# Loading half of one batch's q in pieces of unequal height, in a sliding-window attention and spectral-mix kernel

## The chip, the cores and the metric

The kernel runs on one core of one Trainium2 chip. The metric is the device time of one execution, in microseconds. Five engines work side by side: TensorE (PE in the profile, with its weight loads as PEld), VectorE (DVE), ScalarE (ACT), GpSimd (POOL) and the sync engine (SP). Data come from HBM into SBUF by DMA transfers. Here GpSimd issues every transfer that converts float32 to bfloat16 on the way, and SP issues the first load of k and all stores. Sixteen DMA engines carry out the transfers.

## What is computed

q, k and v have 8 batches, 8 heads, 576 positions and 64 channels. A causal attention with a window of 64 positions gives x of 8 x 576 x 512. Then a Fourier mixing along the positions with 64 modes, each with two 512 x 512 float32 matrices, and a last channel product:

```python
    mask = (rel >= 0) & (rel < window)
    scores = np.where(mask, scores, -1000000000.0)
    ...
    return np.matmul(attn, v).astype(np.float32)
...
    X = np.fft.rfft(x, axis=1)
    Xr, Xi = (np.real(X[:, :n_modes]), np.imag(X[:, :n_modes]))
    Yr = np.einsum('bmd,mde->bme', Xr, w_r) - np.einsum('bmd,mde->bme', Xi, w_i)
    Yi = np.einsum('bmd,mde->bme', Xr, w_i) + np.einsum('bmd,mde->bme', Xi, w_r)
    Y[:, :n_modes] = Yr + 1j * Yi
    y = np.fft.irfft(Y, n=S, axis=1)
    u = x + y
    return (u + np.maximum(u @ w_ch, 0.0)).astype(np.float32)
```

The matrices `w_r` and `w_i` are 134 MB of float32, q, k and v together 28 MB. All of it is read from HBM once (the imaginary matrix of mode 0 is not needed).

## The kernel before

**Stages.** The attention runs first, batch after batch, in windows of 512 score columns (`NWIN` windows, the loop over `w`). While it runs, the first matrices of the mixing are loaded into every buffer that is free: `wls`, 13 early tiles, and then the attention's own buffers as they are given up (`spare`). At some 141 us the mixing begins: `half(i)` multiplies one 512 x 512 matrix with the spectra of all batches (line 618), and `issue(i)` loads the matrices that follow into a ring of buffers as they come free. The inverse transform and the channel product are laid between these steps. After the last matrix come the last products, additions and stores.

**The loads of q, k and v.** `load(b, which)` (lines 109 to 112) brings one batch's q, k or v into a raw tile of 128 partitions. `runs` (line 107) cuts the batch into 256 rows of 18 positions x 64 channels, 4,608 bytes of float32 each, and puts two of them, numbered by x, on each partition: row (g p) of the first four heads is x = 0, of the last four x = 1. There are two raw tiles of each kind, so the load of batch b + 2 waits for the transposes of batch b; `refill` places the loads and the early matrices in GpSimd's order. The last load of all is q of batch 7, and behind it on GpSimd stand matrices alone.

**The transposes.** `transpose_units(b)` turns the raw tiles by PE: `part` transposes six pieces of 64 channels for each x (line 247) into one PSUM tile, with `ident_bf` as the matrix that PE multiplies by, and copies the result out by ACT or DVE (line 58 or 59). The three units of q are the units 6, 7 and 8 of a batch.

**Order on the queues.** PE and GpSimd run in the order in which the program is written (`manual_schedule`); DVE and ACT are placed by the scheduler in the attention. GpSimd's transfers take eight completion semaphores in turn (DMASW0 to DMASW7 in the program's list of instructions). Each transfer waits, besides what its buffer asks for, for the semaphore that the transfer eight places earlier has used.

The lines that hold the loads of the matrices and the wait of the first q unit:

```python
        nc.gpsimd.dma_start(out=wt, in_=src[m].rearrange("(p c) e -> p c e", c=NC))
...
                        nc.tensor.transpose(out=ps[64 * hh:64 * hh + 64, c, :],
                                            in_=src[:, hh, (c0 + c) * D:(c0 + c + 1) * D],
                                            identity=ident_bf)
```

Of the kernel before, what the change touches and what calls it, by code (L numbers as in the profile page):

```python
# [11 lines left out]
BF16 = mybir.dt.bfloat16  # L12
# [8 lines left out]
def view(ap, off, dims):  # L21

    return bass.AP(ap.tensor, ap.offset + off, [list(ap.ap[0])] + [list(d) for d in dims])
# [3 lines left out]
def kernel(  # L27
# [10 lines left out]
    nc = tc.nc  # L38
    B, H, S, D = q.shape
# [8 lines left out]
    RUN = S // 32  # L48
# [6 lines left out]
    def evac(o, i, on_act):  # L55

        if on_act:
            return nc.scalar.copy(out=o, in_=i)  # L58
        return nc.vector.tensor_copy(out=o, in_=i)  # L59
# [10 lines left out]
    ident_bf = consts.tile([128, 128], BF16, name="ident_bf")  # L70
# [19 lines left out]
    acons = p1.enter_context(tc.tile_pool(name="acons", bufs=1, side="right"))  # L90
# [10 lines left out]
    RAW = {"k": k, "q": q, "v": v}  # L101

    def raw_tile(which):
        return rawp.tile([128, 2, RUN * D], BF16, name="r" + which)

    def runs(b, which):
        return RAW[which][b].rearrange("(x g) (p c) d -> (g p) x (c d)", g=4, c=RUN)

    def load(b, which):
        r = raw_tile(which)  # L110
        nc.gpsimd.dma_start(out=r, in_=runs(b, which))
        raws[b, which] = r


# [63 lines left out]
    with tc.manual_schedule(engines=ALL_FOUR):  # L178
# [3 lines left out]
        with tc.tile_pool(name="tmpf", bufs=1, side="right") as tmp:  # L182
            mo = tmp.tile([128, NM], FP32, name="mo")
            to = tmp.tile([128, NT], FP32, name="to")
            nc.gpsimd.iota(mo, pattern=[[1, NM]], base=0, channel_multiplier=0,
                           allow_small_or_imprecise_dtypes=True)
            nc.gpsimd.iota(to, pattern=[[128, NT]], base=0, channel_multiplier=1,
                           allow_small_or_imprecise_dtypes=True)
            nc.gpsimd.memset(ident, 0.0)
            nc.gpsimd.affine_select(out=ident, in_=ident, compare_op=ALU.not_equal, fill=1.0,  # L190
                                    base=0, pattern=[[-1, 128]], channel_multiplier=1)
            load(0, "q")
            load(0, "v")
            for t0, t1 in ((0, 3), (3, NT)):
                n = t1 - t0
                mt = tmp.tile([128, 2, n * NM], FP32, name="mtf")
                nc.vector.tensor_tensor(out=view(mt, 0, [[NM, n], [1, NM]]), in0=view(mo, 0, [[0, n], [1, NM]]),
                                        in1=view(to, t0, [[1, n], [0, NM]]), op=ALU.mult)
                gen_trig(tmp, mt, n * NM, trigF[:, t0:t1, 0:NM], trigF[:, t0:t1, NM:2 * NM], "f")
                if t0 == 0:  # L200
                    nc.vector.tensor_copy(out=ident_bf, in_=ident)
        nc.scalar.activation(out=spark, in_=ident[:, 0:1], func=ACT_F.Exp)
        raws[0, "k"] = raw_tile("k")
        for c, engine in enumerate((nc.vector, nc.gpsimd, nc.vector)):
            cc = slice(6 * D * c, 6 * D * (c + 1))
            engine.tensor_copy(out=raws[0, "k"][:, :, cc], in_=k_first[:, :, cc])
        load(1, "k")
        for i in range(4):
            half = i % 2
# [24 lines left out]
    def transpose_units(b):  # L234

        rk, rq, rv = (raws.pop((b, which)) for which in "kqv")
        qT = qtp.tile([128, 4, S], BF16, name="qT")
        vT = vtp.tile([128, 4, S], BF16, name="vT")
        kT, vt = kTs[b % 2], vts[b % 2]
        qTs[b] = qT  # L240

        def part(src, dst, c0, on_act):
            def f():
                ps = ps_misc.tile([128, 6, 128], BF16, name="pst", tag="misc")
                for c in range(6):
                    for hh in range(2):
                        nc.tensor.transpose(out=ps[64 * hh:64 * hh + 64, c, :],  # L247
                                            in_=src[:, hh, (c0 + c) * D:(c0 + c + 1) * D],
                                            identity=ident_bf)
                evac(view(dst, c0, [[S, 4], [RUN, 32], [1, 6]]),  # L250
                     view(ps, 0, [[32, 4], [1, 32], [128, 6]]), on_act)
            return f

        def vback(u):
            def f():
                ps = ps_misc.tile([128, 6, 128], BF16, name="psv", tag="misc")
                for i in range(6):
                    a, j = divmod(6 * u + i, 9)
                    if j == 4:
                        parts = [(0, 64, 2 * a, 512), (64, 64, 2 * a + 1, 0)]  # L260
                    else:
                        parts = [(0, 128, 2 * a + (j > 4), 128 * j - (j > 4) * S)]
                    for r0, n, g, t0 in parts:
                        nc.tensor.transpose(out=ps[r0:r0 + n, i, :],  # L264
                                            in_=vT[:, g, t0:t0 + n], identity=ident_bf)
                evac(view(vt, 6 * u * VW, [[18 * VW, 2], [VW, 6], [1, D]]),
                     view(ps, 0, [[D, 2], [128, 6], [1, D]]), u != 1)
                if u:
                    hs = slice(u - 1, u + 2, 2)
                    nc.vector.tensor_copy(out=vt[64:128, 1, hs, 1:9], in_=vt[64:128, 0, hs, 0:8])  # L270
                    nc.vector.tensor_copy(out=vt[0:64, 1, hs], in_=vt[0:64, 0, hs])
            return f

        return [part(rk, kT, 0, True), part(rk, kT, 6, False), part(rk, kT, 12, True),
                part(rv, vT, 0, False), part(rv, vT, 6, True), part(rv, vT, 12, False),
                part(rq, qT, 0, True), part(rq, qT, 6, False), part(rq, qT, 12, True),
                vback(0), vback(1), vback(2)]

    def head_of(n):
# [143 lines left out]
    with tc.manual_schedule(engines=ALL_FOUR):  # L423
        first = transpose_units(0)
        for j in (0, 1, 2, 6, 7, 8):
            first[j]()
            refill(0, j)
            if j in (2, 8):
                warm_up(3)
        for half in range(2):  # L430
            pp = slice(64 * half, 64 * half + 64)
            nc.vector.tensor_copy(out=band2[pp], in_=band[pp, half, :])
        mask(0, 1)
        scores(0)
        for j in (3, 4, 5):
            first[j]()
            refill(0, j)
            warm_up(2)
        for vt in vts:
            nc.vector.memset(vt[:, 0, :, :, 64:66], 1.0)  # L440
        for j in (9, 10, 11):
            first[j]()
            refill(0, j)
        nc.vector.memset(pso, 1.0)
        nc.vector.tensor_copy(out=ident_r, in_=ident)
    with tc.manual_schedule(engines={E.PE, E.Pool}):
# [9 lines left out]
        def unit(b, j):  # L456
            if b not in units:
                units[b] = transpose_units(b)
            units[b][j]()
            refill(b, j)  # L460
            turned(b, j)

        for w in range(NWIN + 1):
# [5 lines left out]
            n = len(todo)  # L469
# [16 lines left out]
            if w in (NWIN - 4, NWIN - 1):  # L486
                i = (B - 2) % 2 if w == NWIN - 4 else (B - 1) % 2
                spare(kTs[i])
                spare(qtp.tile([128, 4, S], BF16, name="qT"))
            if w in (NWIN - 4, NWIN):  # L490
                i = (B - 2) % 2 if w == NWIN - 4 else (B - 1) % 2
# [386 lines left out]
    for k, (f, delta, n, few) in enumerate(items):  # L878
        i = S_I + k * (T_I - 2 - S_I) // len(items)
# [25 lines left out]
    with tc.manual_schedule(engines=ALL_FOUR):  # L905
# [92 lines left out]
        for k in range(6):  # L998
# [10 lines left out]
                              in_=view(psys[0], 0, [[2 * B, NC], [2, B], [1, 2]]))  # L1009
# [78 lines left out]
```

## Time and profile before

| what | us |
|---|---|
| median of 3 runs | 425.69 (425.55 to 426.05) |
| the profiled execution | 425.65 |
| its span, first to last instruction | 423.8 |
| PE busy | 352.3 (83%) |
| DVE, ACT, POOL busy | 189.2, 159.8, 81.6 |
| weight loads of PE (beside its products) | 233.6 |
| last transfer of a matrix issued, landed | 375.98, 390.39 |

The span is divided into 40 slices of 10.6 us; the profile gives for each the busy share of every engine, the mean busy share of the sixteen DMA engines and the rate in bytes written. A transfer of 512 KB (bfloat16 as written) is one matrix, 1 MB of float32 as read. "To landing" is the time from an issue to the last of the transfer's sixteen completions, one from each DMA engine. The trace also holds each completion and each packet with its queue, start and size, but not its engine. The profiled run's granted clock of PE is 0.84 of full speed on the mean.

### The profile page before, as it was taken

What the parts mean: (1) busy time and instruction counts of PE and PEld (TensorE: products, weight loads), DVE (VectorE), ACT (ScalarE), POOL (GpSimd) and SP (SyncE); (2) the same over time, 40 slices, a digit from 0 to 9 for tenths busy, and PEclk for the clock granted to TensorE, in tenths of its full rate; (3) what the DMA queues carried; (4) which work ended last, traced back from release to release, by engine and by line L of the source; (5) the groups of instructions that cost most, each with busy time, mean ns of one, the idle gap of its engine ahead of it and who ended that gap; (6) DMA issues with size and microseconds to landing.
All of it is one profiled execution on the core that took longest, in us unless ns stands there. A gap on an engine that the chain in (4) does not pass through costs nothing.

```text
span 423.8 us, 11438 instructions
## 1 busy us (share of the span) xinstructions
PE 352.3 (83%) x5156; PEld 233.6 (55%) x5185; DVE 189.2 (45%) x359; ACT 159.8 (38%) x267; POOL 81.6 (19%) x146
## 2 busy tenths in 40 slices
PE   7799999999997779866669587767789899998994
PEld 3466656656654567644446455545556565554451
DVE  6676775766764001634332351121104345340895
ACT  5565766767754100122102110110023343330863
POOL 6322222221031130411112012120121112200000
PEclk9999999999999555966756656666579999999997
DMA  8999999999999999999999999999999999995598
GB/s 212 211 214 212 214 212 212 213 213 213 214 214 214 213 215 261 215 214 214 215 214 213 215 213 215 215 213 215 213 215 214 214 213 211 214 214 106 203 370 320
DMA packets 29920, 92.55 MB, mean 218 GB/s; under 512 B 2352, under 2 KB 2352, under 8 KB 29872
## 3 DMA queue, kind: packets, MB, share of 16 engines
q0 software_dynamic: 24624, 81.21, 95.9%
q1 hardware_dynamic: 5248, 10.62, 6.8%
q8 instruction: 40, 0.66, 0.6%
q14 instruction: 8, 0.07, 0.0%
HBM read 162.53 MB, written 9.44 MB: 406 GB/s over the span
## 4 chain that ended last, share of the span: by engine, by line
PE 42%; DMA 39%; DVE 7%; issue 5%; ACT 3%; POOL 0%; DVEq 0%; POOLq 0%; ACTq 0%
DMA wms<-in_moe_w_r_dram 20%; DMA wms<-in_moe_w_i_dram 19%; PE psy L618 7%; PE pso L343 6%; PE pst L247 5%; PE psv L264 3%; PE psx L365 3%; PE pss L963 3%; DVE x_sb L351 2%; PE pss L956 2%; PE pss L300 2%; PE pss L319 2%; PE psy L903 2%; DVE vT L59 2%; PE psf L800 1%
## 5 line engine op out<-in xcount | busy, mean ns | idle before, releaser
L759 PE MATMUL psz<-wch,xT 128*128 128x512 f32 x144 | 65.0, 594 | 0.0
L753 DVE CAST xT<-pxt 128x1024 fp32r<-128x1024 bf16 x18 | 22.0, 1224 | 78.0 <-PE pxt L748 78.0
L762 ACT CAST Z<-psz 128x1024 fp32r<-128x1024 f32 x18 | 18.2, 1012 | 102.2 <-PE psz L759 94.5
L325 ACT ACTIVATE et<-pss 128x512 bf16<-128x512 f32 x72 | 39.2, 599 | 13.7 <-PE pss L319 13.7
L618 PE MATMUL psy<-XQ,wls 128*128 128x16 bf16 x560 | 22.0, 192 | 23.7 <-DMA wls<-in_moe_w_r_dram 14.2
L759 PEld LDWEIGHTS psz<-wch,xT 128*128 128x128 f32 x144 | 37.4, 287 | 5.9
L618 PE MATMUL psy<-XQ,wms 128*128 128x16 bf16 x624 | 25.1, 192 | 17.9 <-DMA wms<-in_moe_w_i_dram 12.7
L618 PEld LDWEIGHTS <-wls 128*128 128x128 bf16 x560 | 19.5, 106 | 33.8 <-DMA wls<-in_moe_w_r_dram 17.4
L618 PEld LDWEIGHTS <-wms 128*128 128x128 bf16 x624 | 21.4, 103 | 30.2 <-DMA wms<-in_moe_w_i_dram 15.3
L343 PE MATMUL pso<-vt,et 128*64 128x65 bf16 (+1 forms) x576 | 32.3, 203 | 3.5 <-DVE x_sb L351 1.6
L811 DVE TENSOR_TENSOR Z<-pse,Z 128x1024 fp32r<-128x1024 f32 x16 | 19.6, 1225 | 29.3 <-PE pse L800 29.3
L343 PEld LDWEIGHTS <-et 128*64 128x64 bf16 (+1 forms) x576 | 22.2, 109 | 14.2 <-issue 6.7
L351 DVE TENSOR_TENSOR x_sb<-pso,rcp 128x640 bf16<-128x640 f32 x32 | 26.3, 822 | 0.9
L618 PE MATMUL psy<-XQ,wt 128*128 128x16 bf16 x560 | 20.5, 192 | 4.8 <-DMA wt<-in_moe_w_i_dram 2.3
L618 PEld LDWEIGHTS <-wt 128*128 128x128 bf16 x560 | 18.3, 104 | 11.2 <-DMA wt<-in_moe_w_i_dram 4.3
L59 DVE CAST YT<-psy 128x256 fp32r<-128x256 f32 x6 | 2.5, 424 | 42.0 <-PE psy L618 32.7
L59 DVE COPY vT<-pst 128x768 bf16<-128x768 bf16 x16 | 15.3, 958 | 12.9 <-PE pst L247 11.3
L981 ACT ACTIVATE pss<-pss 128x512 f32<-128x512 f32 x35 | 18.5, 581 | 4.7 <-PE pss L963 4.1
L300 PE MATMUL pss<-band,ident_bf 64*64 64x512 bf16 x120 | 16.5, 396 | 0.0
L264 PE MATMUL psv<-ident_bf,vT 128*128 128x128 bf16 (+1 forms) x160 | 15.6, 226 | 0.6 <-DVE vT L59 0.6
L58 ACT COPY vt<-psv 128x768 bf16<-128x768 bf16 x16 | 12.9, 807 | 8.3 <-PE psv L264 8.2
L58 ACT COPY qT<-pst 128x768 bf16<-128x768 bf16 x16 | 12.9, 813 | 6.4 <-PE pst L247 6.4
(191 smaller groups left out, 605.7 us busy)
## 6 DMA issues: line engine op xcount, KB each, us to landing
wt<-in_moe_w_i_dram POOLq DMA_DIRECT2D x19, 512.0 KB, 20.4
wt<-in_moe_w_r_dram POOLq DMA_DIRECT2D x16, 512.0 KB, 19.4
wls<-in_moe_w_r_dram POOLq DMA_DIRECT2D x8, 1024.0 KB, 21.8
wms<-in_moe_w_i_dram POOLq DMA_DIRECT2D x7, 1024.0 KB, 22.2
wms<-in_moe_w_r_dram POOLq DMA_DIRECT2D x7, 1024.0 KB, 21.6
wls<-in_moe_w_i_dram POOLq DMA_DIRECT2D x6, 1024.0 KB, 21.3
rq<-in_q_dram POOLq DMA_DIRECT2D x8, 576.0 KB, 15.3
rv<-in_v_dram POOLq DMA_DIRECT2D x8, 576.0 KB, 13.8
```

Of the source, the lines that this page charges most:

```text
L58: return nc.scalar.copy(out=o, in_=i)
L59: return nc.vector.tensor_copy(out=o, in_=i)
L247: nc.tensor.transpose(out=ps[64 * hh:64 * hh + 64, c, :], in_=src[:, hh, (c0 + c) * D:(c0 + c + 1) * D], identity=ident_bf)
L264: nc.tensor.transpose(out=ps[r0:r0 + n, i, :], in_=vT[:, g, t0:t0 + n], identity=ident_bf)
L300: nc.tensor.matmul(out=pss[(2 * w + hh) % 3][64 * half:64 * half + 64, :], lhsT=ident_bf[pp, pp], rhs=view(band[pp], 128 * half, [[0, WIN ...
L325: nc.scalar.activation(out=et[:, hh, :], in_=pss[(2 * w + hh) % 3], func=ACT_F.Exp, scale=EX_SCALE)
L343: nc.tensor.matmul(out=pso[po, hh, block(b, i // 2) * VW:block(b, i // 2) * VW + D + 1], lhsT=et[pk, hh, col:col + 64], rhs=vt[pk, 1 - f % ...
L351: nc.vector.tensor_tensor(out=view(x_sb, b * NT * DM + g * D, [[4 * D, 2], [DM, NT], [1, D]]), in0=view(pso, 0, [[512, 2], [VW, NT], [1, D]]),
L618: nc.tensor.matmul(out=view(psy, off + 2 * B * e, [[1, 2 * B]]), lhsT=w[:, c, 128 * e:128 * e + 128], rhs=XQ[:, m // HM, c, :, 1 - im:3 - ...
L753: nc.vector.tensor_copy(out=o, in_=i)
L759: nc.tensor.matmul(out=psz[s][:, j, :], lhsT=xts[s % 2][0][:, j, 128 * c:128 * c + 128], rhs=wch[:, c, :], start=(c == 0), stop=(c == NC - 1))
L811: nc.vector.tensor_tensor(out=z, in0=ps, in1=z, op=ALU.add)
```

## The change

The load of q of batch 7 (`BY_PARTS`) becomes eight transfers. The 128 rows of x = 0 are taken by six: (parts, rows of each part) are (5, 2), (2, 2), (2, 2), (4, 2), (3, 2) and (4, 24), with source rows dealt to the parts in turn, so that the rows land on the partitions in another order. A seventh, `aside`, brings 24 pieces of 16 values, as 12 parts of 2, into a tile that nothing reads. The eighth brings the 128 rows of x = 1 as before, in one. The transposes of batch 7's q for x = 0 use `back`, a matrix with the columns of `ident_bf` in the order that undoes the shuffle; six DVE copies build it. The list of instructions shows GpSimd with seven transfers more in the place of this load and else the same order, DVE with the six copies placed early, behind the second product of the first table of sines, PE with the same number of instructions, and the first q unit of batch 7 waiting for the six part transfers' semaphores and for that of the eighth transfer in place of one. Everything behind takes the semaphore one place earlier in the cycle of eight.

```diff
+    BY_PARTS = (B - 1, "q")
+    PARTS = ((5, 2), (2, 2), (2, 2), (4, 2), (3, 2), (4, 24))
+    REST = 12
+    assert sum(n * m for n, m in PARTS) == 128 and (sum(n for n, m in PARTS) + REST) % 16 == 0
+    aside = acons.tile([2 * REST, 16], BF16, name="aside")
+    back = acons.tile([128, 128], BF16, name="back")
+
+    def parts_of(ap):
+        at = 0
+        for n, m in PARTS:
+            yield at, n * m, ap[at:at + n * m].rearrange("(r a) c -> a r c", a=n)
+            at += n * m
+
     def load(b, which):
         r = raw_tile(which)
-        nc.gpsimd.dma_start(out=r, in_=runs(b, which))
+        if (b, which) == BY_PARTS:
+            halves = [RAW[which][b, x * H // 2:(x + 1) * H // 2].rearrange("g (p c) d -> (g p) (c d)", c=RUN)
+                      for x in range(2)]
+            for at, n, src in parts_of(halves[0]):
+                nc.gpsimd.dma_start(out=r[at:at + n, 0, :], in_=src)
+            nc.gpsimd.dma_start(out=aside, in_=halves[0][:2 * REST, 0:16].rearrange("(r a) c -> a r c", a=REST))
+            nc.gpsimd.dma_start(out=r[:, 1, :], in_=halves[1])
+        else:
+            nc.gpsimd.dma_start(out=r, in_=runs(b, which))
         raws[b, which] = r
...
-        def part(src, dst, c0, on_act):
+        def part(src, dst, c0, on_act, by_parts=False):
             def f():
                 ps = ps_misc.tile([128, 6, 128], BF16, name="pst", tag="misc")
+                if by_parts and c0 == 0:
+                    at = 0
+                    for n, m in PARTS:
+                        nc.vector.tensor_copy(out=view(back, at, [[1, n], [n, m]]),
+                                              in_=view(ident_bf, at, [[m, n], [1, m]]))
+                        at += n * m
                 for c in range(6):
                     for hh in range(2):
                         nc.tensor.transpose(out=ps[64 * hh:64 * hh + 64, c, :],
                                             in_=src[:, hh, (c0 + c) * D:(c0 + c + 1) * D],
-                                            identity=ident_bf)
+                                            identity=back if by_parts and hh == 0 else ident_bf)
...
-                part(rq, qT, 0, True), part(rq, qT, 6, False), part(rq, qT, 12, True),
+                *(part(rq, qT, 6 * i, i != 1, (b, "q") == BY_PARTS) for i in range(3)),
```

## The prediction

> **What bounds the kernel now.** I read the page's slices first, then the queues and the chain, then GpSimd's timeline around the changed load.
>
> ```profile
> span 423.8 us, 11438 instructions
> ...
> DMA  8999999999999999999999999999999999995598
> GB/s 212 211 214 212 214 212 212 213 213 213 214 214 214 213 215 261 215 214 214 215 214 213 215 213 215 215 213 215 213 215 214 214 213 211 214 214 106 203 370 320
> ...
> q0 software_dynamic: 24624, 81.21, 95.9%
> ...
> q8 instruction: 40, 0.66, 0.6%
> ...
> PE 42%; DMA 39%; DVE 7%; issue 5%; ACT 3%; POOL 0%; DVEq 0%; POOLq 0%; ACTq 0%
> ```
>
> The DMA engines never pause from the first slice to the 36th and write at 211 to 215 GB/s whatever PE does (the 261 is the one unconverted load). So the end is the last matrix's landing at 390.39 us plus a tail of 33 us of work and stores. PE's 42% of the chain does not speak against it: in the attention PE is busy without setting the end, since the matrices queue in front of the DMA engines whatever it does. A stretch in which the DMA engines lack work is lost for good; work taken off the latest of them is won.
>
> They are not equal. Every transfer has sixteen landings in the trace. At 103.94 us eight engines are 1.75 to 2.29 us ahead of the last; at 390.39 us eight are 4.86 to 5.87 us ahead, the others 0 to 1.23. The 40 packets of q8 (16 KB, PE's instructions) explain it: their durations repeat with a period of eight (893, 893, 948, 945, 935, 974, 974, about 1,000 ns), and after each one one engine's landings come some 0.6 us later. So eight engines fetch instructions in turn and are late, and the other eight are not.
>
> ```profile
> 84.99 0.57 POOL L138 DMA_DIRECT2D wt<-in_moe_w_i_dram  x1
> 87.78 0.70 POOL L111 DMA_DIRECT2D rq<-in_q_dram  x1 [2.23 <-PE pst L247]
> 88.84 0.56 POOL L138 DMA_DIRECT2D wt<-in_moe_w_i_dram  x1 [0.36 <-DMA wt<-in_moe_w_i_dram]
> 91.28 0.54 POOL L138 DMA_DIRECT2D wt<-in_moe_w_r_dram  x1 [1.88 <-DMA rq<-in_q_dram]
> 93.74 0.53 POOL L138 DMA_DIRECT2D wt<-in_moe_w_r_dram  x1 [1.92 <-DMA wt<-in_moe_w_r_dram]
> 96.58 0.53 POOL L138 DMA_DIRECT2D wt<-in_moe_w_i_dram  x1 [2.31 <-DMA rk<-in_k_dram]
> ```
>
> This is the place of the change (columns: start, duration, engine and line, output and input, idle time before and what ended it). From 88.84 us on GpSimd waits for landings, not for buffers. Those waits are the eight semaphores: the transfers eight places earlier landed at 88.55, 91.00, 93.45 and 96.30, and each issue follows by 0.28 or 0.29 us. No more than eight transfers can be in flight here, and with eight of full size that is some 20 us of work.
>
> **The change part by part.** *Eight issues for one.* The first part goes out at 87.78 as now. The next seven take the semaphores whose last users land at 88.55, 91.00, 93.45, 96.30, 98.74, 101.97 and 103.94 in the trace. With 0.28 each, the part of 24 rows goes out at 99.02, `aside` at 102.25 and the half of x = 1 at 104.22. Behind it wait the matrices that now go out from 88.84 on; nothing but GpSimd's own transfers is queued there. At 103.94 us all that was issued before q has landed, and what is left in the queue are the parts. Eight small transfers fill the eight places that held 20 us of work, and the DMA engines run dry.
>
> How long: a row of 4,608 bytes takes an engine 174 ns (packets of the first k load, one engine's starts at 4.296, 4.470, 4.644 us). If the rows go as the shapes say, four engines have 26 rows of the parts (4.52 us) and twelve have 2 (0.35 us). So the last ordinary engine is idle from 104.29 until the half's rows flow. The trace has no transfer issued by GpSimd into an empty queue. From below: SP's first store went out at 395.91 and its first packet ran at 396.76, 0.85 us. From above: the first q load, issued at 1.60, ran its first packets at 5.32 when the engines had finished k, at most 3.7 us. Between them, and the nearest row, since it reads HBM: SP's k load went out at 0.74, its first packet ran at 1.82, and the engines had done its 16 rows at 5.45 on the mean; less 16 x 0.174 = 2.78 that is an effective start at 2.67, 1.93 us after the issue. GpSimd's issue is 0.1 us longer (0.53 against 0.43). I take 2.0: effective start 106.2 (105.07 to 107.9), the half's 8 rows 1.39, q landed at 107.6 against 106.79 now, 0.8 us late.
>
> That is for the engine that was last at 103.94. The idle stretch also takes from the others what they were ahead. The engine that lands last at 390.39 is the one of the fetch at 380.99, the 39th; its earlier fetches are those at 106.12 and at 55.61, so at 103.94 it was the least late of its eight, 0.95 us ahead. It would have ended q at 103.94 - 0.95 + 2.78 = 105.77 and now does at 107.59: 1.8 us late, with the saving of six rows (1.04) already in it. Its fetch at 106.12 now meets an engine just starting, which can hide up to 0.6. I take 0.1 off: **+1.7 us**. After that the queue fills within some 3 us (four matrices by 106.5, 9.8 us of work), and nothing gives the time back, as the slices show no later gap.
>
> *`back`.* Six copies on DVE, at most the 0.22 us of the 128 x 128 cast beside them: 1.3 us, against 0.34 us of idle time before 3.90 and 0.93 before 5.99 (waiting for k). Nothing; with that cover gone 0.1 us on the first transposes, themselves covered by 7.5 us and more of transfers in flight.
>
> *Transposes and waits.* The same instructions with another matrix. They run at
>
> ```profile
> 115.94 0.53 PE L247 MATMUL pst<-ident_bf,rq 128*64 128x128 bf16 x12
> ```
>
> 8 us after the half and some 7 after the latest heavy part (108.5), so the wait for seven semaphores costs nothing; if q came later than that, scores and the next windows of the attention would stand behind it.
>
> *`aside`.* 24 packets in the dry stretch: nothing (in a full queue perhaps 0.05 us).
>
> Sum: 423.8 + 1.7 = 425.5 span, 425.65 + 1.7 = 427.35 for that run, which lies 0.04 below the median: 427.4.
>
> The Trainium skill ("DMA: Bandwidth & Descriptors", section "Anatomy of one DMA — SWDGE (gpsimd) path") gives a transfer a fixed part of about 2.0 us. No run here shows it for GpSimd alone; taken for the restart it is the same 427.4.
>
> **The rivals.** *The heavy part falls on engines that fetch.* For them the part is no idle stretch but 26 + 8 rows against 16: 3.13 us more. The one that is last at the end gives +3.1, 428.8; if the four are the others of the eight, 0.6 to 1.2 ahead at the end, the last is at +1.9 to +2.5, 427.6 to 428.2. For it: eight of sixteen fetch, and no row tells which sixteen-part place these have. Against: four neighbours could be free of them.
>
> *Faster.* Twelve engines have six rows less, 6 x 0.174 = 1.04 us. If the four heavy ones are among those 4.86 us and more ahead, that is won wherever the queue doesn't run dry: 424.6. It decides at an effective start of 104.4, 0.2 us after the half's issue. Against it stands the 0.85 us of the quickest start in the trace.
>
> *Covered.* The end doesn't follow the DMA stream, or the start comes within 0.9 us: 425.7. Against: no slice with a gap.
>
> *Not what it says.* The parts may be spread evenly over all sixteen engines. The ordinary engines still run dry, until the same 106.2: +1.7, as forecast.
>
> *Every transfer pays.* Under 64 KB "you're paying mostly overhead", the Trainium skill says (same page, section "Rules for kernel authors"). By the rows: an ending matrix and the next are 2.45 us apart with no gap, so the price is hidden in a full queue; if each of seven paid the 1.93 us of the k load by itself on the DMA engines, 13.5 us, 439.
>
> **How the numbers follow.** A difference within 0.2% (0.85 us) can't be told from none. Forecast, with the even spread, 0.55; heavy part on fetching engines 0.32; faster 0.05; covered 0.06; every transfer pays 0.02. The start's bounds give the forecast 426.4 (0.68 late) to 429.2; the second case reaches 428.8. The upper bound is a row that only limits, so the range ends near the second case: 426.4 to 428.9. Slower: 0.55 and 0.32 less some 0.03 for a quick start, and 0.02: 0.86. Faster 0.05, same 0.09.
>
> **What would show it.** GpSimd's issues at the times above, waiting for DMA, with the half at 104.2 and the next matrix after it; a dip in the DMA row and in GB/s in the tenth slice (95 to 106 us); q's half landing at about 107.6; the last matrix at 392.1. A half issued well before 104, or no dip, makes the forecast wrong; so does a last landing before 390.4. A last matrix at 393 or later with four landings behind the rest speaks for the heavy part on fetching engines.

## The result and the profile after

The changed kernel takes 427.11 us (median of 6 runs, 426.96 to 427.36) where the kernel before takes 425.59 (6 runs, 425.35 to 426.05): +1.52 us, a ratio of 1.0035 (95% interval 1.0022 to 1.0048). The profiled run is one of 427.16 us. These are the first lines of its page, those that answer to the ones shown of before:

```profile
span 425.4 us, 11484 instructions
...
DMA  8999999998999999999999999999999999996598
GB/s 213 211 213 213 213 212 214 212 213 162 204 214 213 215 213 261 215 214 214 213 215 214 214 214 215 215 214 215 213 215 214 212 215 214 212 214 136 201 370 318
...
q0 software_dynamic: 25184, 81.21, 95.7%
```

The span is 1.6 us longer. The tenth slice (96 to 106 us) has fallen from 213 to 162 GB/s and the eleventh from 214 to 204; no other of the first 36 is more than a few GB/s off. The last matrix lands at 391.88 us, where it landed at 390.39: 1.49 us later, so nearly the whole difference is there before the last matrix is used. GpSimd's timeline at the changed load (columns: start, duration, engine and line, output and input, idle time before and what ended it):

```profile
88.41 1.26 POOL L131 DMA_DIRECT2D rq<-in_q_dram  x2 [2.23 <-PE pst L277]
91.84 0.55 POOL L131 DMA_DIRECT2D rq<-in_q_dram  x1 [2.17 <-DMA rq<-in_q_dram]
94.31 0.58 POOL L131 DMA_DIRECT2D rq<-in_q_dram  x1 [1.92 <-DMA wt<-in_moe_w_r_dram]
97.17 0.55 POOL L131 DMA_DIRECT2D rq<-in_q_dram  x1 [2.28 <-DMA rk<-in_k_dram]
99.61 0.67 POOL L131 DMA_DIRECT2D rq<-in_q_dram  x1 [1.90 <-DMA wt<-in_moe_w_r_dram]
102.33 0.57 POOL L132 DMA_DIRECT2D aside<-in_q_dram  x1 [2.05 <-DMA rv<-in_v_dram]
104.88 0.56 POOL L133 DMA_DIRECT2D rq<-in_q_dram  x1 [1.98 <-DMA wt<-in_moe_w_i_dram]
105.44 0.57 POOL L162 DMA_DIRECT2D wt<-in_moe_w_i_dram  x1
105.97 1.09 POOL L162 DMA_DIRECT2D wt<-in_moe_w_r_dram  x2
107.01 0.58 POOL L162 DMA_DIRECT2D wt<-in_moe_w_i_dram  x1
```

L131 issues the parts, L132 `aside`, L133 the half of x = 1, L162 the matrices. The first two parts go out together. Each small transfer behind them waits about 2 us for the landing of another transfer and goes out alone, so that the half is issued 16.5 us after the first part. Then GpSimd stops waiting: four matrices follow in 2.2 us, because the first five parts have landed by 105.37 and their places are free. A run of issues without a bracket says by itself only that places are free.

That the queue is empty too shows in the view of the DMA queues from 102 to 112 us, in which one character, or one number, stands for 0.25 us. Before:

```profile
DMA  9997999999999999999999999999999899999999
GB/s 216 225 218 151 246 182 212 212 252 195 227 190 225 216 230 198 266 239 180 213 213 213 197 229 197 229 197 197 246 197 229 180 229 229 229 197 213 197 213 229
```

Changed kernel:

```profile
DMA  8987667558332222796899999999996999979999
GB/s 145 173 137 119 87 123 115 83 84 140 56 56 46 55 55 55 92 120 92 157 221 194 210 218 175 222 199 189 231 229 131 213 213 213 229 148 246 197 246 213
```

From 104.5 us to 106.0 the engines write 46 to 56 GB/s and are busy 0.2 to 0.3: a quarter of the 213, that is four engines of sixteen. Before 104.5 the busy share sinks to 0.5: engines that were ahead have run out already. The packets say the same: from 104.87 to 106.13 us only four engines move rows, 173 ns apart. The Trainium skill ("DMA: Bandwidth & Descriptors", section "Why a DMA increments its semaphore by 16 and not by 1") says that a transfer issued by GpSimd that is divided over k < 16 engines runs on k neighbours, taken from a cursor that goes round; the four busy engines agree with the number k, while which engines they are the trace doesn't hold.

### The profile page after: what moved, and what is told of

Same layout as the page of the kernel before. It is cut to its first block, busy times and chain, and to the rows that moved or that the text cites. A ratio compares the mean times of both kernels' runs of the same rounds, so it can differ in the third digit from the quotient of the medians.

```text
span 425.4 us, 11484 instructions
## 1 busy us (share of the span) xinstructions
PE 355.8 (84%) x5185; PEld 233.5 (55%) x5185; DVE 189.0 (44%) x365; ACT 160.0 (38%) x267; POOL 85.7 (20%) x153
## 4 chain that ended last, share of the span: by engine, by line
PE 47%; DMA 37%; DVE 6%; issue 3%; ACT 3%; POOL 1%; DVEq 0%; POOLq 0%; ACTq 0%
DMA wms<-in_moe_w_i_dram 20%; DMA wms<-in_moe_w_r_dram 12%; PE psy L648 7%; PE pso L373 6%; PE pst L277 6%; DMA wls<-in_moe_w_i_dram 5%; PE psv L294 3%; PE psx L395 3%; PE pss L993 3%; PE pss L330 2%; PE pss L986 2%; PE pss L349 2%; DVE x_sb L381 2%; PE psy L933 2%; PE psz L789 2%
## 5 line engine op out<-in xcount | busy, mean ns | idle before, releaser
L789 PE MATMUL psz<-wch,xT 128*128 128x512 f32 x144 | 61.9, 570 | 0.0
L789 PEld LDWEIGHTS psz<-wch,xT 128*128 128x128 f32 x144 | 35.1, 270 | 5.5
L933 PE MATMUL psy<-trigF,ident_bf 128*128 128x512 bf16 x46 | 17.9, 454 | 0.0
```

The costliest lines, as they stand in the source:

```text
L789: nc.tensor.matmul(out=psz[s][:, j, :], lhsT=xts[s % 2][0][:, j, 128 * c:128 * c + 128], rhs=wch[:, c, :], start=(c == 0), stop=(c == NC - 1))
L933: nc.tensor.matmul(out=o, lhsT=ident_bf, rhs=view(trigF, 0, [[1, DM]]), start=True, stop=True)
```

## The experiments

The disputed points were two: whether the eight places in flight are what costs the time, and on which engines the part of 24 rows falls. For the second, the parts are counted from the place where the round of sixteen stands. All transfers in front of them have sixteen parts, so it is taken to stand the same in all these kernels; the change's part of four is at places 0 to 3 of it (5 + 2 + 2 + 4 + 3 = 16). The kernel before ran beside each group: median 425.60 us for the first four, 425.54 for the next two, 425.70 for e7 to e10, 425.60 for e11.

**e1_even: the same eight transfers, every engine the same rows.**

```diff
-    PARTS = ((5, 2), (2, 2), (2, 2), (4, 2), (3, 2), (4, 24))
-    REST = 12
+    PARTS = ((16, 1), (16, 1), (16, 1), (16, 1), (16, 2), (16, 2))
+    REST = 16
```

> Six transfers of 16, 16, 16, 16, 32 and 32 rows, all in sixteen parts, then aside (16 parts) and the half of x = 1: eight transfers in the same places as the changed kernel's, but every DMA engine has the same 8 rows of the first half. Theory (eight small transfers take the eight semaphores, the queue runs dry): the half goes out at 104.2 to 104.9 us and the time is the changed kernel's, 427.1, within 0.4. Rival (the uneven rows cost the time): 425.6, as before.

Measured: 426.97 us (426.75 to 427.77, 7 runs), ratio 1.0029 (1.0018 to 1.0040). Its page:

```profile
GB/s 211 211 213 212 214 213 212 213 212 165 206 214 213 214 214 261 215 214 214 213 214 215 214 214 214 214 215 214 214 214 214 214 213 213 214 214 122 198 370 320
```

The dip is in the same two slices (165 and 206), and the half goes out at 104.75. So the unequal parts are not needed for the loss: eight small transfers do it.

**e2_tiny7: the kernel before, and behind its whole load of q seven transfers of 1 KB.** They put next to no work on the DMA engines (packets of 24 or 25 ns); they take places.

```diff
         nc.gpsimd.dma_start(out=r, in_=runs(b, which))
+        if (b, which) == (B - 1, "q"):
+            for n in range(7):
+                tiny = acons.tile([32, 16], BF16, name=f"tiny{n}")
+                src = RAW[which][b, 0, 32 * n:32 * n + 32, 0:16]
+                nc.gpsimd.dma_start(out=tiny, in_=src)
```

> The kernel before, with seven tiny transfers (32 rows of 16 values each, into tiles that nothing reads) behind the last load of q, which stays whole. No row is moved and no order restored. Theory: the next matrix waits for the semaphore of q itself, which lands at 106.8, goes out at 107.1 and flows 1.7 to 2.0 us later, when all engines have been idle: 2.9 to 3.2 us late for the engine that ends last, less up to 0.6 for a fetch that falls in the gap: 428.0 to 428.8. Rival (small transfers cost only their own time in the queue, some 0.1 us): 425.7.

Measured: 428.49 us (428.06 to 429.03, 4 runs), ratio 1.0065 (1.0052 to 1.0079). GpSimd's timeline and, below it, the DMA queues from 102 to 112 us:

```profile
104.74 0.49 POOL L116 DMA_DIRECT2D tiny<-in_q_dram  x1 [1.97 <-DMA wt<-in_moe_w_i_dram]
107.59 0.55 POOL L143 DMA_DIRECT2D wt<-in_moe_w_i_dram  x1 [2.36 <-DMA rq<-in_q_dram]
```

```profile
DMA  9998999999756467442210000009800899989999
```

The next matrix is the ninth transfer counted from the load of q, and it goes out 0.28 us after q's landing at 107.31. From 107.5 to 108.75 the engines stand at 0; the matrix's first packets come 1.26 us after its issue. Nothing else was computed or moved, and 2.9 us are lost: the places alone are enough.

**e3_heavy0: few transfers, the heavy part at places 0 to 3.** Three transfers in all, and no `aside`. Four engines get 26 rows of x = 0, twelve get 2, as in the change.

```diff
-    PARTS = ((5, 2), (2, 2), (2, 2), (4, 2), (3, 2), (4, 24))
-    REST = 12
+    PARTS = ((4, 26), (12, 2))
...
-            nc.gpsimd.dma_start(out=aside, in_=halves[0][:2 * REST, 0:16].rearrange("(r a) c -> a r c", a=REST))
```

> The changed kernel with the same division, 26 rows on the same four engines and 2 on the other twelve, but in two transfers ((4, 26), (12, 2)) and without aside: three transfers in the place of one, so five large ones stay in flight and the queue does not run dry. Theory, if the four engines are free of instruction fetches: 1.04 us faster than before, 424.6 (424.3 to 424.9). If one or more of the four fetch: 1.9 to 3.1 slower than before, 427.5 to 428.7. Rival (the uneven rows or the restored order cost time by themselves): 427.1 as the changed kernel.

Measured: **424.60 us** (424.48 to 425.10, 10 runs), ratio 0.9977 (0.9968 to 0.9986), faster than both. GpSimd's timeline:

```profile
88.65 1.27 POOL L129 DMA_DIRECT2D rq<-in_q_dram  x2 [2.23 <-PE pst L274]
91.28 0.57 POOL L130 DMA_DIRECT2D rq<-in_q_dram  x1 [1.37 <-DMA rq<-in_q_dram]
93.76 0.54 POOL L159 DMA_DIRECT2D wt<-in_moe_w_i_dram  x1 [1.90 <-DMA wt<-in_moe_w_r_dram]
```

The matrices follow from 93.76 on, at the old distance, and no slice dips (the tenth and eleventh have 210 and 215 GB/s). The four heavy engines land together at 106.70, within 0.32 us. Twelve engines have six rows less, and that is worth 1.0 us to the end.

**e4_heavy8, e5_heavy4, e6_heavy12: the same with the heavy part at places 8, 4 and 12.**

```diff
+    PARTS = ((8, 2), (4, 26), (4, 2))    # e4
+    PARTS = ((4, 2), (4, 26), (8, 2))    # e5
+    PARTS = ((12, 2), (4, 26))           # e6
```

> As e3_heavy0 with the 26 rows on the four engines that stand eight places later: ((8, 2), (4, 26), (4, 2)), four transfers in the place of one, no dry queue. If the engines that fetch are eight neighbours opposite to those of e3_heavy0, 1.9 to 3.1 slower than before (427.5 to 428.7), with the last landing at 392.3 or later; if these four are free of fetches, 424.6. A time equal to before would mean that rows moved between engines don't matter.

> As e3_heavy0 with the 26 rows on the four engines four places later: ((4, 2), (4, 26), (8, 2)), no dry queue. If none of these four fetches, 424.6; if one or more fetch, 427.5 to 428.7. With eight fetching neighbours that hold the places 8 to 11, either this or e6_heavy12 is slow as a whole, or both hold some fetching engines and are slow.

> As e3_heavy0 with the 26 rows on the last four places: ((12, 2), (4, 26)), no dry queue. If none of these four fetches, 424.6; if one or more fetch, 427.5 to 428.7. If the fetching engines are the places 8 to 15, this is slow and e5_heavy4 is fast.

Measured: e4 428.67 us (428.40 to 428.78, 4 runs; ratio 1.0068, 1.0054 to 1.0082), e5 428.18 (428.00 to 428.40, 3 runs; 1.0061, 1.0039 to 1.0084), e6 428.80 (428.52 to 428.81, 3 runs; 1.0072, 1.0049 to 1.0095). The engines at the end, in the view of the DMA queues from 384 to 394 us, 0.25 us a character: before, e3 and e4, one fence each.

```profile
DMA  8666554456554555535420000000000000020000
```

```profile
DMA  8785979769885767331000000000000030000000
```

```profile
DMA  9999999999996636545442201222021222000000
```

Before: the busy share falls to a half by 385, and that half of the engines goes on to 389. e3: the engines run out almost together, and the last is earlier. e4: a few, at 0.1 to 0.2, work alone for some 3 us, and the last of them lands at 393.10. Counting the late landings at the end, or in e5 behind q, gives the fetching engines among the four places: 0 at places 0 to 3, 2 at 4 to 7, 3 at 8 to 11, 3 at 12 to 15. That is eight, as many as the trace of before had shown, and where the part sits decides 4 us.

**e7_seven and e8_six: the change with one and two transfers less**, the same rows for each engine, `aside` and half left in.

```diff
-    PARTS = ((5, 2), (2, 2), (2, 2), (4, 2), (3, 2), (4, 24))
+    PARTS = ((5, 2), (4, 2), (4, 2), (3, 2), (4, 24))    # e7
+    PARTS = ((9, 2), (4, 2), (3, 2), (4, 24))            # e8
```

> The changed kernel with two of its small transfers made one, (2, 2) and (2, 2) into (4, 2): same rows on the same engines, seven transfers in the place of one. Theory: the half goes out at about 102.3, the next matrix at about 104.5 and flows 1.7 us later, as in the changed kernel, at 105.9 to 106.6; the engine that ends last has done its parts and the half at 104.7 and would have begun that matrix at 105.8 in the kernel before: 0.1 to 0.8 late, 425.7 to 426.4. Rival (each transfer costs its own share: 2.5 us between the changed kernel and e3_heavy0 over five transfers, 0.5 each): 426.6.

> The same with six transfers, (9, 2), (4, 2), (3, 2), (4, 24), aside and the half. Theory: the next matrix goes out at about 102.3 and flows from 104.0, before the engine that ends last has done the half (104.7): no dry queue, 424.6 as e3_heavy0. Rival (0.5 us for each transfer): 426.1.

Measured: e7 425.95 us (425.66 to 427.31, 10 runs; ratio 1.0013, 1.0003 to 1.0023), e8 424.78 (424.52 to 425.03, 10 runs; 0.9978, 0.9969 to 0.9987). GpSimd's timelines, e7 and then e8:

```profile
102.27 0.56 POOL L133 DMA_DIRECT2D rq<-in_q_dram  x1 [2.19 <-DMA rv<-in_v_dram]
104.78 0.54 POOL L162 DMA_DIRECT2D wt<-in_moe_w_i_dram  x1 [1.94 <-DMA wt<-in_moe_w_i_dram]
```

```profile
99.39 0.56 POOL L133 DMA_DIRECT2D rq<-in_q_dram  x1 [1.90 <-DMA wt<-in_moe_w_r_dram]
102.15 0.54 POOL L162 DMA_DIRECT2D wt<-in_moe_w_i_dram  x1 [2.19 <-DMA rv<-in_v_dram]
```

With seven, the first matrix behind q goes out at 104.78, when the half and the heavy part are the only work left; the tenth slice has 188 GB/s. With six, it goes out one landing earlier and the slice has 205. By the medians the price falls by 1.2 us for each of the two transfers taken away and then stops (e7's ten runs lie between 425.66 and 427.31, so the single step is less sure than the two together), for three transfers (e3) are no better than six by more than 0.2 us. (e7's profile is of a run of 426.9 us, about 1 us above its median.)

**e11_between: all eight transfers of the change, with three matrices issued among them**, behind the second, fourth and sixth part.

```diff
-            for at, n, src in parts_of(halves[0]):
+            for i, (at, n, src) in enumerate(parts_of(halves[0])):
                 nc.gpsimd.dma_start(out=r[at:at + n, 0, :], in_=src)
+                if i % 2:
+                    early(1)
```

> The changed kernel's eight transfers, every row on the same engine, in the same order among themselves, but three of the four matrices that wait behind them are issued in between (after the second, fourth and sixth). Theory (it is the dry queue, not the number of transfers nor their rows): two large transfers stay in the queue at 104 us, it does not run dry, and the saving of six rows comes out: 424.6 to 424.9, as e3_heavy0 and e8_six. Rival (eight transfers cost their share wherever they stand): 427.1.

Measured: 425.01 us (424.59 to 425.30, 11 runs), ratio 0.9984 (0.9975 to 0.9993). GpSimd's timeline:

```profile
91.70 0.59 POOL L164 DMA_DIRECT2D wt<-in_moe_w_i_dram  x1 [2.18 <-DMA rq<-in_q_dram]
...
99.46 0.55 POOL L164 DMA_DIRECT2D wt<-in_moe_w_r_dram  x1 [1.87 <-DMA wt<-in_moe_w_r_dram]
...
104.72 0.67 POOL L131 DMA_DIRECT2D rq<-in_q_dram  x1 [1.98 <-DMA wt<-in_moe_w_i_dram]
105.39 0.57 POOL L164 DMA_DIRECT2D wt<-in_moe_w_r_dram  x1
...
107.15 0.57 POOL L135 DMA_DIRECT2D rq<-in_q_dram  x1 [0.63 <-DMA wt<-in_moe_w_i_dram]
```

The half of x = 1 goes out even later than in the change, at 107.15, and costs nothing, since matrices lie in front of the engines meanwhile (212 and 202 GB/s in the two slices). It waits for the matrix issued at 91.70, eight places earlier; the small transfers had that one and the next to hide behind. The time is 0.1 us above the range expected, and 2.1 us below the change with the same parts.

**e9_both5 and e10_both7: could more rows be moved?** Both halves by parts, with the other matrix in all transposes and no `aside`. e9 gives the heavy parts to places 0 to 4; e10 was meant to give them to places 0 to 4, 7 and 8, with two matrices between the halves.

```diff
+    PARTS = ((5, 19), (11, 3))                     # e9
+    PARTS = ((5, 17), (2, 1), (2, 17), (7, 1))     # e10
...
+            for x in range(2):
+                if x:               # e10 only
+                    early(2)
+                for at, n, src in parts_of(halves[x]):
+                    nc.gpsimd.dma_start(out=r[at:at + n, x, :], in_=src)
```

> Both halves of q with 19 rows on each of the first five places and 3 on the other eleven, in four transfers ((5, 19), (11, 3) twice), no aside, the restored order for both halves. The sizes 5, 2, 2, 4, 3 of the change, and the counts of heavy engines that landed late in e4_heavy8 (three), e5_heavy4 (two) and e6_heavy12 (three), fit fetching engines at 5, 6, 9 to 12 and two of 13 to 15. If place 4 is free: 10 rows less for the fetching engines, 1.74 us, and 22 more (3.8 us) for five that were 4.9 to 5.9 ahead: 1.0 to 1.7 faster than before, 423.9 to 424.6. If place 4 fetches: 22 rows more on it, 3.2 to 3.8 slower, 428.8 to 429.4.

> Both halves with 17 rows on each of the places 0 to 4, 7 and 8 and one row on the other nine ((5, 17), (2, 1), (2, 17), (7, 1) twice), with two of the waiting matrices issued between the halves so that the queue does not run dry. If 7 and 8 are free of fetches too: 14 rows less for the fetching engines (2.4 us) and 18 more (3.1 us) for the seven: 1.7 to 2.4 faster than before, 423.2 to 423.9. If 7 or 8 fetches: 2.5 to 3.1 slower than before, 428.1 to 428.7.

Measured: e9 424.91 us (424.65 to 425.16, 11 runs; ratio 0.9980, 0.9971 to 0.9989), e10 426.42 (426.01 to 430.09, 11 runs; 1.0026, 1.0009 to 1.0044). Both are misses. e9 is 0.3 us above its range and no better than e3. At its end fifteen landings are 1.0 us and more ahead of the last one, so a single engine sets the end now; probably one of the five with 22 rows more (3.8 us at 174 ns), which no run separated. Place 4 does not fetch, or e9 would have gone the way of e4. e10 fits neither of the two times expected of it, and its trace shows that it did not do what was meant. Behind the first half two landings at 109.78 stand 1.5 us and more behind the rest, as of two heavy engines that fetch. One matrix later they are still the last, at 112.22. With 17 rows of the second half (2.96 us) they would have landed at 115.2, but the last landing of that half is at 113.67. So its heavy rows lie on other engines than those of the first half. In e9 the same five engines take both: they land last behind each half, four of them 0.43 to 0.85 us ahead of the fifth, at the same distances both times. Parts of one row, (2, 1) and (7, 1), are what e10 has and e9 hasn't; whether these leave the round elsewhere, no run separated. So e10 is no test of places 7 and 8, nor of the order of the change's sizes (5, 2, 2, 4, 3) from which they were guessed, and that its profiled run took 428.06 us, next to one of the expected times, says nothing. Its runs spread over 4 us. Why it varies so stays open.

## Why the prediction was right

It said 427.4 us for the reason that the runs bear out: eight small transfers take the eight places, and the DMA engines run dry. That the sum lies within 0.3 us of 427.11 is in part luck, since its terms were off in opposite directions.

*The bound.* The DMA engines set the end: of +1.52 us, 1.49 are there at the last landing, and the time follows the last landing: e3 389.75, before 390.39, change 391.88, e4 393.10, and each of these profiled runs takes 35.3 us more than that.

*The eight places.* Shown by e2, which adds places and nothing else, and by the row of 8, 7, 6 and 3 transfers: +1.5, +0.3, -0.9 and -1.0 us against before. e11 shows that the number as such is not it: eight transfers with work between them cost nothing. The issues predicted for the part of 24 rows, `aside` and the half were 99.02, 102.25 and 104.22 us; they were 99.61, 102.33 and 104.88, so the half went out 0.66 us late. The last transfer in front of q had landed 0.65 us later than before (104.59 against 103.94). That began long before the parts: PE's first q transposes took 2.13 us instead of 1.20 at 9 us, and the durations of the fetches follow in another turn. It isn't the price of `back`, for in e2, which has none, that landing is at 104.46, and in the other ten kernels between 104.14 and 104.52. What sets it off stays open.

*The restart: a term that was mis-sized.* I took 2.0 us from the issue of the half to an effective start, between 0.85 and 3.7. Its first packets ran at 106.155, 1.27 us after the issue at 104.88, and the twelve engines that were done first ended its rows at 107.96 on the mean; less 8 x 0.174 that is 106.57, 1.69 us after the issue. So the issue was 0.66 us later and the restart 0.31 us shorter than in the sum, and the rows began to flow at 106.57 instead of 106.2. Yet the last matrix landed 0.2 us earlier than forecast (391.88 against 392.1), so the engine that ends last lost less than the sum has for it; which engine that is, the trace doesn't tell. One sign was missed: the half was to land at about 107.6. Fifteen engines landed between 108.06 and 108.75, the last one at 109.74, 1.0 us behind them. e1 has such an engine too (109.36, 0.96 us behind the others). What holds it up stays open. The fixed part of about 2.0 us of the Trainium skill ("DMA: Bandwidth & Descriptors", section "Anatomy of one DMA — SWDGE (gpsimd) path") holds the handling of the completion too, which the 1.69 us don't hold; so it was no measure for this term, though the sum by it came out the same.

*The lead that is lost.* The idle stretch was to take from the engines what they were ahead. At 104.59 eight landings are 2.4 to 3.2 us ahead of the last; behind the dry stretch all are within about 1.7. Without the saving the loss is 427.11 less the 424.60 of e3, 2.5 us, where the prediction had 1.7 + 1.04 = 2.7. How much of it is the gap of the last engine and how much the lost lead, no run separates.

*The saving of six rows.* Taken as 1.04 us; e3 measured 1.0. The change doesn't get it: e1, which saves no rows, is 1.4 us slower than before, and the change, which saves six on twelve engines, 1.5. Behind a dry stretch the engines start again almost together, and what they had saved ahead of it doesn't count. The prediction had this, with the same time for an even spread.

*`back`, the transposes, `aside`.* DVE's and PE's timelines of the changed kernel:

```profile
3.48 0.62 DVE L272 COPY back<-ident_bf 128x10 bf16<-128x10 bf16 x6
...
6.04 1.65 DVE L230 CAST rk<-x_sb 128x768 bf16<-128x768 f32 x2 [0.95 <-DMA x_sb<-in_k_dram]
```

```profile
116.57 0.24 PE L277 MATMUL pst<-back,rq 128*64 128x128 bf16 x1
```

The six copies take 0.62 us, and DVE still waits 0.95 us for k behind them. The first transpose of q runs without a wait, 6.8 us after the half's landing at 109.74. e8, which keeps `aside`, is 0.18 us above e3, which has none; their intervals overlap, so nothing of it can be told.

*The rivals.* The heavy part on fetching engines had 0.32. It fell: e3 puts it where the change does and is fast, and in the change itself the part landed by 107.34, where 24 rows more would have taken the eight rear engines, which landed between 103.62 and 105.37 just before, to 107.8 and later. No row of before spoke for it that these four engines are free, so that part of the forecast was luck. The rival's price was right, though, at 428.2 to 428.8 us in e4, e5 and e6, which don't run dry, against 427.6 to 428.8. The faster case had 424.6 us if the queue didn't run dry: e3 and e8. "Every transfer pays" falls with e8 and e11, which issue six and eight transfers and are faster than before. An even spread falls with the four busy engines, but its time was as argued (e1: 426.97). A gap covered elsewhere falls with the last landing.

## What to carry to other kernels

Where a queue is kept full by a fixed number of transfers in flight, count what each transfer takes of these places, not only its bytes: here six transfers in a row cost nothing that shows (424.78 us against 424.60 with three), while eight emptied the queue and cost 2.5 us against the same rows in three. Put large transfers between small ones, or use fewer parts. And when the end hangs on the latest of the DMA engines, look at each transfer's sixteen landings: rows moved from late engines to early ones gave 1.0 us in e3, while four engines chosen wrongly lost 3.

## What the runs showed of the hardware beyond that

The engines that fetch instructions are no block of neighbours: among places 0 to 3, 4 to 7, 8 to 11 and 12 to 15 there are 0, 2, 3 and 3. A transfer that GpSimd issues to idle engines had its first packet after 1.27 us here and after 1.26 us in e2. And engines lose their lead where the queue runs dry: in the change the eight early engines end 2.1 to 3.9 us ahead of the last, where before they ended 4.9 to 5.9 ahead.
